# Joining small-matmul bursts in slice 1 of a chunked linear attention with a two-layer MoE: one core of a Trainium2 chip

## The chip, the core and the metric

The kernel runs on one core of one Trainium2 chip. The metric is the device time of one execution in microseconds, the median of several runs. The engines are TensorE (PE for matmuls, PEld for weight loads), VectorE (DVE), ScalarE (ACT), GpSimd (POOL) and SyncE (SP), whose queue issues all DMAs.

## What is computed

Cut to what matters; all data are float32.

```python
# q, k, v: (4, 8, 768, 64), lam: (8,), blocks of 64 positions
for b in range(12):
    intra = (qb @ kb.T * Dmask) @ vb            # Dmask: lam ** (i - j) below the diagonal
    inter = (qb * lam ** (pos + 1)) @ kv_state
    out[b] = intra + inter
    kv_state = lam ** 64 * kv_state + (kb * lam ** (63 - pos)).T @ vb
x = out, as (3072, 512)
g = relu(x @ w_in) ** 2                          # w_in: (512, 2048)
y = g @ w_out                                    # w_out: (2048, 512)
```

## The kernel before

**Chunks and slices.** The 3072 tokens are 24 chunks t of 128 (two blocks of one batch entry for all 8 heads, 6 chunks to a batch entry). Four chunks make a slice m of 512 tokens. For a slice the MoE runs over 16 pieces f of the hidden width: `hidden` multiplies, `positive` and `square` (ScalarE) take relu and square, `rest` (VectorE) gets the square's lower half, and `project` adds the piece into four accumulators. To keep the accuracy each operand is split into an upper half that fp32r holds and a lower half, and three products are added: 12 matmuls of 128x128 by 128x512 for `hidden`, 12 for `project`. A stretch of the loop is named here by the chunks whose attention it does: slice 1 is the loop at m = 0, in which the MoE of the first four chunks runs beside the attention of chunks 4 to 7; slice 2 is the loop at m = 1, with the attention of chunks 8 to 16 beside it. The last slices use fewer products and their own loop.

**Attention of a chunk** is made of small matmuls of 64x64: `scores` (32), `news` (32, what the chunk adds to the state, 16 for the last chunk of a batch entry) and `result` (64, of the masked scores with v and of q with the state). Beside them: `prep_k` and `prep_q` (GpSimd, L492 and L487) scale k and q, `masked` (VectorE, L498 whole or L505 in halves) multiplies the scores by the mask, `fade` (ScalarE, L539) and `advance` (VectorE, L329) or `state` (L521) carry the state on in a ring of three slots, `copy_qx` and `copy_vx` (ScalarE) move rows across, and `attend` with `split` (L593 and L594) puts a result into upper and lower halves for the next slice.

**The step of slice 1.** Each chunk has four steps f, step = f % 4. In step 0 `look` issues scores and news of chunk t = 4 + f // 4 behind the projection, in step 1 they are masked and the state is advanced, in step 2 `result` is issued between the hidden product and the projection, and `attend` follows. Both use a pool of two PSUM banks (`ps_a`). In slice 2 `burst` does scores of t, result of t - 1 and news of t in one run of small matmuls, with two banks of its own (`ps_b`) and a third from the pool of the hidden products (`ps_h`, 2 banks); `keep` takes the result out in two pieces.

**The weights** are rounded on the fly in slice 1, a unit u = f + 2 (two blocks of 128x512) in a step: `first` (ScalarE, L234 and L239), `clamp` (L247), `shift` (L251), `sign` (L258), `rounded` (L264) on VectorE, then in the next step `upper` (ScalarE, L273) and `lower` (L278). Unit f + 1 must be there for the hidden product f + 1. In steps 1 and 2 VectorE does half of `lower` and GpSimd the other (L281), behind a tiny copy `turn` (L285) that waits for VectorE's half. `wload` (L220) issues a unit's loads three units ahead; a unit's raw space is free after its rounding.

**Order.** Nothing reorders: each engine, and SyncE's queue of DMAs, works in the order in which the body issues. One step of slice 1 issues on VectorE: masking and the first state block (step 1), clamp, shift, sign, lower, the second state block (step 1), rounded, rest, and the attention's lower half (step 2).

Of the kernel before, what the change touches and what calls it, by code (L numbers as in the profile page):

```python
# [7 lines left out]
F32 = mybir.dt.float32  # L8
# [35 lines left out]
def body(ctx: ExitStack, tc: tile.TileContext, qT, kT, kvq, lam, w, out):  # L44
# [52 lines left out]
    chunk = {}  # L97

    def place(t):
        if t in (2, 3):  # L100
            x = wk.tile([P, KT * C, 4], F32, name=f"lent{t}", tag=("xh", "xl")[t - 2])
            x = x.rearrange("p a b -> p (a b)")
        else:
            x = sets[t % 2 if t == 1 or 2 * G < t < SOLO else 0].bitcast(F32)
        c = chunk[t] = {}
        for i, n in enumerate(("k", "v", "q", "kf") if t < 2 * G else ("k", "q", "kf", "v")):
            c[n] = x[:, i * DM : (i + 1) * DM]
        c["all"] = x[:, 0 : 3 * DM]
        if t >= 2 * G:
            c["kq"] = x[:, 0 : 2 * DM].rearrange("p (a b) -> p a b", a=2)  # L110
        if t > SOLO and t % 2:
            c["v"] = v_other
# [363 lines left out]
        return o  # L476

    def keep(t, o):
        x = by_pair(held[t // G % 2], t)
        for y in range(2):  # L480
            nc.scalar.copy(x[:, y], o[y].rearrange("p (a i) -> p a i", a=2))

    def prep_q(t):
        n = slice(0 if t % NCB else 1, 2)
# [7 lines left out]
        nc.gpsimd.tensor_tensor(out=x, in0=x, in1=y.broadcast_to([P, NPR, 2, D]), op=ALU.mult)  # L492

    def masked(t):
        a = a_of[t] = a_last[0] if t > (PLAIN + 2) * G else wk.tile([P, 2, 2, 2, L], F32, name="a", tag="a")
        x, w_ = sc_of.pop(t), mask.rearrange("p j a i -> p j (a i)")
        if t < 2 * G:
            V.tensor_tensor(  # L498
                out=a.rearrange("p j b a i -> p j b (a i)"),
                in0=x.rearrange("p j (b n) -> p j b n", b=2),  # L500
                in1=w_.unsqueeze(2).broadcast_to([P, 2, 2, 2 * L]), op=ALU.mult,
            )
            return
        for j in range(2):
            V.tensor_tensor(  # L505
                out=a[:, j].rearrange("p b a i -> p b (a i)"),
                in0=x[j].rearrange("p (b n) -> p b n", b=2),
                in1=w_[:, j].unsqueeze(1).broadcast_to([P, 2, 2 * L]), op=ALU.mult,
            )
# [17 lines left out]
            else:  # L527
                nc.scalar.copy(new, u)

    faded = {}  # L530

    def fade(t, b):
        n = 2 * t + b
        if b == 0:
            faded[t] = wk.tile([P, 2, 4, D], F32, name="faded", tag="a")
        if n % (2 * NCB) and b < len(u_of[t]):
            old = before_block(n).rearrange("p a j d -> p (a j) d")
            for g in range(4):
                nc.scalar.activation(faded[t][:, b, g], old[:, g], AF.Identity, scale=fd[:, g : g + 1])  # L539

    def advance(t, b):
        if b < len(u_of[t]):
            n = 2 * t + b
            new = before_block(n + 1).rearrange("p a j d -> p (a j d)")
            if n % (2 * NCB):
                add(new, u_of[t][b], faded[t][:, b].rearrange("p g d -> p (g d)"))
            else:
                V.tensor_copy(new, u_of[t][b])
        if b:
            del u_of[t], faded[t]  # L550

    def result(t, banks, begun=(), keys=range(2)):
        g = Group(banks, begun, keys)
# [368 lines left out]
    ps_acc = ctx.enter_context(tc.tile_pool(name="ps_acc", bufs=G, space=PSUM))  # L922

    prev = None
    for m in range(PLAIN):
        if m == 0:
            new_x(1)
        else:
            middle.close()
            ps_b = ctx.enter_context(tc.tile_pool(name="ps_b", bufs=1, side="right", space=PSUM))  # L930
            held += [
                wk.tile([P, KT, N], F32, name=f"held{k}", tag=n) for k, n in enumerate(("xh", "xl"))
            ]
        for f in range(NF):
            h = hidden(m, f, *xs_of[m])
            if m == 0:
# [1 line left out]
                step = f % 4  # L938
                u_ = f + 2
                if step == 2:  # L940
                    o = two_banks(ps_a, "att")
                    result(t, of(o))
                    if t + 1 < 2 * G:
                        load(t + 1)
                        load_vx(t + 1)
                    else:
                        for n in (t + 1, t + 2):
                            load_kq(n)
                            load_v(n)
# [46 lines left out]
            else:  # L996
                t = 2 * G + f
                if f == 0:
                    prep_k(t)
                if f <= 2 * G:  # L1000
                    x = burst(t, f > 0, True, lambda: positive(h))
                    rest(m, f, h, square(h))
                else:
                    squared(m, f, h)
                if 1 <= f <= 2 * G:
                    keep(t - 1, x)
                if f <= 2 * G:
                    masked(t)
                    state(t)
                    if f:  # L1010
# [4 lines left out]
                    prep_k(t + 1)  # L1015
                    copy_vx(t)
                if f - 1 in SUMS:
# [3 lines left out]
                if f <= 2 * G:  # L1021
                    copy_qx(t)
                if f == 2 * G + 1:
                    fetch(0)
# [5 lines left out]
            prev = (m, f)  # L1030

    temp = wk.tile([P, 4, DM], F32, name="temp", tag="xl")
    v_other = wk.tile([P, DM], F32, name="v", tag="a")
    a_last = [wk.tile([P, 2, 2, 2, L], F32, name="a", tag="a")]
    for n in range(2, RING):
        fetch(n)
    for d in range((NM - PLAIN) // 2):
# [97 lines left out]
```

## Time and profile before

| | us |
|---|---|
| median of 3 runs | 585.13 (584.63 to 586.6) |
| profiled execution | 585.56 |
| its span, first to last instruction | 583.8 |
| TensorE busy | 574.4 |
| VectorE busy | 318.9 |
| ScalarE busy | 315.6 |
| GpSimd busy | 81.2 |

Busy time is a sum over the span; a stage in which one engine is full can hide in it. In the order of time a line gives the start, the time from the first start to the last end, engine, line, operation, tiles, shape and count; consecutive records of an engine overlap a little, so that what one costs its engine is read from its start to the next one's. Idle time of an engine before an instruction, with what ended it, stands in brackets; an instruction that was issued and could not yet begin is shown as longer, not as idle time before it. The mean granted TensorE clock is 0.991.

### The profile page before, as it was taken

What the parts mean: (1) busy time and instruction counts of PE and PEld (TensorE: products, weight loads), DVE (VectorE), ACT (ScalarE), POOL (GpSimd) and SP (SyncE); (2) the same over time, 40 slices, a digit from 0 to 9 for tenths busy, and PEclk for the clock granted to TensorE, in tenths of its full rate; (3) what the DMA queues carried; (4) which work ended last, traced back from release to release, by engine and by line L of the source; (5) the groups of instructions that cost most, each with busy time, mean ns of one, the idle gap of its engine ahead of it and who ended that gap; (6) DMA issues with size and microseconds to landing.
All of it is one profiled execution on the core that took longest, in us unless ns stands there. A gap on an engine that the chain in (4) does not pass through costs nothing.

```text
span 583.8 us, 12761 instructions
## 1 busy us (share of the span) xinstructions
PE 574.4 (98%) x5240; PEld 471.4 (81%) x5240; DVE 318.9 (55%) x586; ACT 315.6 (54%) x578; POOL 81.2 (14%) x94
## 2 busy tenths in 40 slices
PE   8899999999999999999999999999999999999997
PEld 5787888888888888888888888888888888888885
DVE  6889999936868676533444333446433333334222
ACT  4589988845656555545655444634344444444221
POOL 7302332331323100011111101000000000000000
PEclk9799999999999999999999999999999999999999
DMA  8667667145998943856555563300354444411001
GB/s 333 224 213 248 227 215 253 61 146 200 300 369 258 349 151 107 274 164 181 183 165 154 151 184 94 122 1 0 118 152 127 126 126 125 120 46 73 1 0 72
DMA packets 51273, 93.62 MB, mean 160 GB/s; under 512 B 4624, under 2 KB 19472, under 8 KB 51216
## 3 DMA queue, kind: packets, MB, share of 16 engines
q1 hardware_dynamic: 51216, 92.82, 49.0%
q8 instruction: 41, 0.67, 0.4%
q14 instruction: 16, 0.13, 0.1%
HBM read 71.83 MB, written 20.97 MB: 159 GB/s over the span
## 4 chain that ended last, share of the span: by engine, by line
PE 98%; DVE 0%; issue 0%; ACT 0%; POOL 0%; DVEq 0%; POOLq 0%
PE h L754 26%; PE acc L648 16%; PE h L612 15%; PE acc L649 15%; PE acc L653 15%; PE h L415 4%; PE b L415 2%; PE att L415 2%; PE att L81 1%; PE open L415 1%; PE h L608 1%; DVE st L521 0%; PE h L366 0%; PE h L378 0%; DVE r L657 0%
## 5 line engine op out<-in xcount | busy, mean ns | idle before, releaser
L648 PE MATMUL acc<-wh,gh 128*128 128x512 f32 x336 | 132.9, 395 | 0.0
L653 PE MATMUL acc<-wh,gl 128*128 128x512 f32 x336 | 131.0, 390 | 0.0
L649 PE MATMUL acc<-wl,gh 128*128 128x512 f32 x336 | 130.9, 390 | 0.0
L648 PEld LDWEIGHTS acc<-wh,gh 128*128 128x128 f32 x336 | 63.0, 188 | 13.8
L653 PEld LDWEIGHTS acc<-wh,gl 128*128 128x128 f32 x336 | 63.1, 188 | 13.3
L649 PEld LDWEIGHTS acc<-wl,gh 128*128 128x128 f32 x336 | 63.1, 188 | 12.6
L633 DVE TENSOR_TENSOR gl<-h,gh 128x512 fp32r<-128x512 f32 x48 | 33.1, 689 | 71.7 <-ACT h L628 71.7
L619 ACT ACTIVATE h<-h 128x512 f32<-128x512 f32 x48 | 28.0, 584 | 77.8 <-PE h L612 44.0
L329 DVE TENSOR_TENSOR temp<-h,temp 128x512 f32<-128x512 f32 x48 | 33.0, 688 | 56.9 <-PE h L754 46.9
L754 PE MATMUL h<-wh,ring 128*128 128x512 f32 x224 | 60.0, 390 | 0.0
L619 ACT ACTIVATE temp<-temp 128x512 f32<-128x512 f32 x16 | 10.1, 632 | 88.6 <-DVE temp L329 88.6
L487 POOL TENSOR_TENSOR qs<-set,qpow 128x512 f32<-128x512 f32 (+1 forms) x21 | 26.5, 1263 | 169.1 <-PE b L415 157.6
L754 PEld LDWEIGHTS h<-wh,ring 128*128 128x128 f32 x224 | 42.0, 188 | 9.0 <-DVE r L329 0.4
L329 DVE TENSOR_TENSOR r<-h,temp 128x512 f32<-128x512 f32 x24 | 16.6, 692 | 34.3 <-PE h L754 33.1
L633 DVE TENSOR_TENSOR gl<-r,gh 128x512 fp32r<-128x512 f32 x24 | 16.6, 691 | 32.9 <-ACT gh L786 32.9
L754 PE MATMUL h<-wl,ring 128*128 128x512 f32 x112 | 34.5, 389 | 0.0
L612 PE MATMUL h<-xh,wh 128*128 128x512 f32 x120 | 33.4, 401 | 0.7 <-ACT xh L593 0.7
L612 PE MATMUL h<-xh,wl 128*128 128x512 f32 x120 | 33.1, 398 | 0.0
L612 PE MATMUL h<-xl,wh 128*128 128x512 f32 x120 | 32.2, 390 | 0.0
L786 ACT CAST gh<-r 128x512 fp32r<-128x512 f32 x24 | 14.9, 621 | 30.0 <-PE acc L649 30.0
L623 ACT ACTIVATE gh<-h 128x512 fp32r<-128x512 f32 x48 | 28.8, 600 | 1.4
L628 ACT ACTIVATE h<-h 128x512 f32<-128x512 f32 x48 | 28.5, 594 | 0.0
(209 smaller groups left out, 1120.9 us busy)
## 6 DMA issues: line engine op xcount, KB each, us to landing
ring<-wd SPq DMA_DIRECT2D x56, 256.0 KB, 2.8
raw<-in_w SPq DMA_DIRECT2D x22, 512.0 KB, 4.7
set<-in_kvq SPq DMA_DIRECT2D x16, 512.0 KB, 3.9
wd<-hl SPq DMA_DIRECT2D x16, 512.0 KB, 5.3
set<-in_kT SPq DMA_DIRECT2D x22, 256.0 KB, 5.0
set<-in_w SPq DMA_DIRECT2D x10, 512.0 KB, 5.1
set<-in_kvq SPq DMA_DIRECT2D x6, 768.0 KB, 6.5
wh<-wd SPq DMA_DIRECT2D x14, 256.0 KB, 2.8
```

What stands on the lines that cost most here:

```text
L329: lambda o, x, y, op=op: V.tensor_tensor(out=o, in0=x, in1=y, op=op)
L415: nc.tensor.matmul(self.banks[row][rows[col], at : at + D], lhsT, rhs, start=key not in self.begun, stop=stop, skip_group_check=True,)
L487: nc.gpsimd.tensor_tensor(out=z, in0=x, in1=w_, op=ALU.mult)
L612: nc.tensor.matmul(h, wt[:, w_in(f), kt * P : (kt + 1) * P], x[:, kt], start=k == 0, stop=k == 11)
L619: nc.scalar.activation(h, h, AF.Relu)
L623: nc.scalar.activation(gh, h, AF.Square)
L628: nc.scalar.activation(h, h, AF.Square)
L633: V.tensor_tensor(out=gl, in0=r, in1=gh.bitcast(F32), op=ALU.subtract)
L648: nc.tensor.matmul(accs[m][i], gh[:, cs], wh[:, j], start=f == 0, stop=False)
L649: nc.tensor.matmul(accs[m][i], gh[:, cs], wl[:, j], start=False, stop=False)
L653: nc.tensor.matmul(accs[m][i], gl[:, cs], wh[:, j], start=False, stop=end)
L754: nc.tensor.matmul(bank, w[:, kw * HALF + kt * P : kw * HALF + (kt + 1) * P], x_slot(2 * c + kt, kx), start=first and q == 0, stop=q == 5, ...
```

## The change

Slice 1 gets `burst` from chunk 5 on: in step 2 of chunk t one burst holds scores of t + 1, result of t and news of t + 1, and the last one takes chunk 8 out of slice 2, which then begins with chunk 9. `look` remains for chunk 4. The pool `ps_b` is opened at f = 2. Masking of t + 1 moves into step 2 and is done in halves; the mask's tile `a` becomes a single one from chunk 4 on. The state is faded straight into its new slot (steps 3 and 0) and added there. `prep_q` of t + 1 moves to step 2, `prep_k` to step 1; chunk 5 is loaded in step f = 1, later chunks in step 2 of the chunk two before, and v of the odd chunks has a tile of its own. `rest` stands ahead of `rounded` in steps 1 and 2. `upper` goes ahead of the burst's ScalarE instructions in step 2.

```diff
+        if t > G and t % 2 and (t < 2 * G or t > SOLO):
+            c["v"] = v_other[0]
...
     def keep(t, o):
+        o = [x.rearrange("p (a i) -> p a i", a=2) for x in o]
+        if t < 2 * G:
+            xh, xl = (by_pair(x, t) for x in xs_of[1])
+            for y in range(2):
+                nc.scalar.copy(xh[:, y], o[y])
+            for y in range(2):
+                sub(xl[:, y], o[y], xh[:, y].bitcast(F32))
+            return
...
     def masked(t):
-        a = a_of[t] = a_last[0] if t > (PLAIN + 2) * G else wk.tile([P, 2, 2, 2, L], F32, name="a", tag="a")
+        a = a_of[t] = a_last[0] if t >= G else wk.tile([P, 2, 2, 2, L], F32, name="a", tag="a")
...
-        if t < 2 * G:
+        if t <= G:
...
     def fade(t, b):
...
-                nc.scalar.activation(faded[t][:, b, g], old[:, g], AF.Identity, scale=fd[:, g : g + 1])
+                nc.scalar.activation(new[:, g], old[:, g], AF.Identity, scale=fd[:, g : g + 1])
...
-                add(new, u_of[t][b], faded[t][:, b].rearrange("p g d -> p (g d)"))
+                add(new, u_of[t][b], new)
...
                 if step == 2:
-                    o = two_banks(ps_a, "att")
-                    result(t, of(o))
-                    if t + 1 < 2 * G:
-                        load(t + 1)
-                        load_vx(t + 1)
-                    else:
-                        for n in (t + 1, t + 2):
-                            load_kq(n)
-                            load_v(n)
-                if step == 1:
+                    if f == 2:
+                        middle.close()
+                        ps_b = ctx.enter_context(
+                            tc.tile_pool(name="ps_b", bufs=1, side="right", space=PSUM)
+                        )
+                    upper(u_ - 1)
+                    x = burst(t + 1, True, True, lambda: positive(h))
+                if f == 1:
+                    load_kq(t + 1)
+                    load_v(t + 1)
+                    wload(u_ + 2)
                     masked(t)
                     advance(t, 0)
...
                 if f > 1:
-                    upper(u_ - 1)
+                    if step != 2:
+                        upper(u_ - 1)
                     lower(u_ - 1, step in (1, 2))
                 if f == 1 or f and step in (0, 3):
                     turn(u_ - 1)
-                if step == 1:
+                if step == 2:
+                    prep_q(t + 1)
+                    if t + 1 < 2 * G:
+                        load_vx(t + 1)
+                    load_kq(t + 2)
+                    load_v(t + 2)
+                    if t + 1 == 2 * G:
+                        load_kq(t + 3)
+                if f == 1:
                     fade(t, 1)
                     advance(t, 1)
-                if f == 0:
+                if step == 3:
+                    fade(t + 1, 0)
+                    advance(t + 1, 0)
+                if step == 0 and f:
+                    fade(t, 1)
+                    advance(t, 1)
+                if f == 0 or step == 1:
                     positive(h)
-                    gh = square(h)
-                    rest(m, f, h, gh)
+                if f == 0 or step in (1, 2):
+                    rest(m, f, h, square(h))
                 if u_ < NLOT:
                     rounded(u_)
-                    wload(u_ + 3)
-                if step == 0 and f:
-                    prep_q(t)
-                if step == 3 and t + 1 < 2 * G:
-                    prep_k(t + 1)
-                if f:
+                    if f:
+                        wload(u_ + 3)
+                if step == 1 or f == NF - 1:
+                    prep_k(t + 1 if step == 1 else t + 2)
+                if f and step not in (1, 2):
                     positive(h)
-                    gh = square(h)
-                    rest(m, f, h, gh)
-                if step == 1:
+                    rest(m, f, h, square(h))
+                if f == 1:
                     copy_qx(t)
                 if step == 2:
-                    attend(t, o)
+                    keep(t, x)
+                    masked(t + 1)
+                if step == 3:
+                    copy_qx(t + 1)
...
-                if step == 0:
+                if f == 0:
                     look(t)
                     fade(t, 0)
             else:
-                t = 2 * G + f
+                t = 2 * G + 1 + f
...
-                if f <= 2 * G:
-                    x = burst(t, f > 0, True, lambda: positive(h))
+                if f < 2 * G:
+                    x = burst(t, True, True, lambda: positive(h))
```

## Rows read from the trace of the kernel before

**Rows 1.** The page: TensorE's busy time (us, share of the span, instructions), and VectorE's busy tenths in 40 equal slices of the span.

```profile
PE 574.4 (98%) x5240; PEld 471.4 (81%) x5240; DVE 318.9 (55%) x586; ACT 315.6 (54%) x578; POOL 81.2 (14%) x94
...
DVE  6889999936868676533444333446433333334222
```

**Rows 2.** The busy time of each engine from 26.50 to 195.14 us, slices 1 and 2 of the loop: the sum over the stretches, and the mean of the 15 stretches.

```profile
sum 168.64, PE 168.61 PEld 137.93 DVE 140.18 ACT 126.47 POOL 48.42; mean PE 11.24 PEld 9.20 DVE 9.35 ACT 8.43 POOL 3.23
```

**Rows 3.** TensorE's order of time: the first four matmuls of hidden products, f = 6 to 10 of slice 1 and f = 3 and 4 of slice 2. A step lasts from one such row to the next.

```profile
66.18 1.07 PE L612 MATMUL h<-xh,wh 128*128 128x512 f32 x4
...
72.94 1.07 PE L612 MATMUL h<-xh,wh 128*128 128x512 f32 x4
...
78.38 1.07 PE L612 MATMUL h<-xh,wh 128*128 128x512 f32 x4
...
85.01 1.19 PE L612 MATMUL h<-xh,wh 128*128 128x512 f32 x4
...
90.58 1.07 PE L612 MATMUL h<-xh,wh 128*128 128x512 f32 x4
...
149.10 1.07 PE L612 MATMUL h<-xh,wh 128*128 128x512 f32 x4
...
156.79 1.07 PE L612 MATMUL h<-xh,wh 128*128 128x512 f32 x4
```

**Rows 4.** VectorE's order of time, f = 10 (a step that shares lower) and the full lower of f = 11 with the rounding behind it; last, ScalarE's second square of f = 10.

```profile
92.98 0.68 DVE L247 TENSOR_SCALAR A<-A 128x1024 f32<-128x1024 f32 x1
93.69 0.69 DVE L251 TENSOR_SCALAR A<-A 128x1024 uint32<-128x1024 uint32 x1
94.42 1.22 DVE L258 SCALAR_TENSOR_TENSOR A<-set,A 128x1024 uint32<-128x1024 uint32 x1
95.56 0.68 DVE L278 TENSOR_TENSOR wl<-third,wh 128x512 fp32r<-128x512 f32 x1
96.16 1.22 DVE L264 CUSTOM_DVE_ANT_0 A<-set,A 128x2048 uint16<-128x2048 uint16 x1
97.30 0.68 DVE L633 TENSOR_TENSOR gl<-h,gh 128x512 fp32r<-128x512 f32 x1
97.89 0.68 DVE L594 TENSOR_TENSOR xl<-att,xh 128x512 fp32r<-128x512 f32 x1
...
101.12 1.22 DVE L278 TENSOR_TENSOR wl<-A,wh 128x1024 fp32r<-128x1024 f32 x1
102.26 1.22 DVE L264 CUSTOM_DVE_ANT_0 A<-raw,A 128x2048 uint16<-128x2048 uint16 x1
...
94.61 0.59 ACT L628 ACTIVATE h<-h 128x512 f32<-128x512 f32 x1
```

**Rows 5.** The order of time at the start of slice 1: VectorE's lower half of unit 4 and TensorE's fourth hidden product, upper and lower weights; the squares' lower half of f = 1, and the first matmuls of the result of chunk 4.

```profile
53.46 1.22 DVE L278 TENSOR_TENSOR wl<-A,wh 128x1024 fp32r<-128x1024 f32 x1
...
53.78 1.07 PE L612 MATMUL h<-xh,wh 128*128 128x512 f32 x4
54.73 1.21 PE L612 MATMUL h<-xh,wl 128*128 128x512 f32 x4
...
44.69 0.68 DVE L633 TENSOR_TENSOR gl<-h,gh 128x512 fp32r<-128x512 f32 x1
...
44.36 0.27 PE L415 MATMUL att<-a,set 64*64 64x64 f32 x2
```

**Rows 6.** The order of time in slice 2: masking in halves (VectorE) and the scaling of q (GpSimd).

```profile
132.21 0.41 DVE L505 TENSOR_TENSOR a<-h,mask 128x256 f32<-128x256 f32 x1
132.54 0.41 DVE L505 TENSOR_TENSOR a<-b,mask 128x256 f32<-128x256 f32 x1
...
138.38 1.29 POOL L487 TENSOR_TENSOR qs<-set,qpow 128x512 f32<-128x512 f32 x1 [9.65 <-PE b L415]
```

**Rows 7.** VectorE and GpSimd in order of time: f = 9, where a state addition stands between lower and rounding, and f = 8, where GpSimd's scaling of q falls beside the squares' lower half.

```profile
89.72 0.42 DVE L329 TENSOR_TENSOR st<-att,faded 128x256 f32<-128x256 f32 x1
90.06 2.39 DVE L264 CUSTOM_DVE_ANT_0 third<-raw,third 128x2048 uint16<-128x2048 uint16 x1
...
89.94 0.17 POOL L285 COPY mark<-wl 1x1 f32<-1x1 f32 x1 [4.12 <-DVE wl L278]
90.08 1.29 POOL L281 TENSOR_TENSOR wl<-A,wh 128x512 fp32r<-128x512 f32 x1
...
85.00 0.68 DVE L633 TENSOR_TENSOR gl<-h,gh 128x512 fp32r<-128x512 f32 x1
...
85.09 0.73 POOL L487 TENSOR_TENSOR qs<-set,qpow 128x256 f32<-128x256 f32 x1
```

**Rows 8.** The same view: the scaling of k and the clamp behind it at f = 11, and the mark of f = 1 with the sign behind it.

```profile
103.48 1.05 POOL L492 TENSOR_TENSOR set<-set,near 128x512 f32<-128x512 f32 x1
...
103.99 1.09 DVE L247 TENSOR_SCALAR third<-third 128x1024 f32<-128x1024 f32 x1
...
41.45 0.58 POOL L285 COPY mark<-wl 1x1 f32<-1x1 f32 x1 [18.34 <-DVE wl L278]
...
42.09 1.23 DVE L258 SCALAR_TENSOR_TENSOR A<-set,A 128x1024 uint32<-128x1024 uint32 x1
```

**Rows 9.** SyncE's queue in order of time, the weight loads from 30.45 us, and a line of the page's DMA issues (KB each, median us from issue to landing).

```profile
30.45 8.39 SPq L220 DMA_DIRECT2D raw<-in_w  x4
...
set<-in_kvq SPq DMA_DIRECT2D x16, 512.0 KB, 3.9
```

More of the change, by code (lines that the diff above doesn't have):

```diff
@@ L96, in body @@
     qpow = const.tile([P, NPR, L], F32, name="qpow")
-    chunk = {}
+    chunk, v_other = {}, [None]
     def place(t):
@@ L110, in place @@
             c["kq"] = x[:, 0 : 2 * DM].rearrange("p (a b) -> p a b", a=2)
-        if t > SOLO and t % 2:
-            c["v"] = v_other
+        else:
+            c["kq"] = x[:, 0 : 3 * DM].rearrange("p (a b) -> p a b", a=3)[:, 0:3:2]
+        if t > G and t % 2 and (t < 2 * G or t > SOLO):
+            c["v"] = v_other[0]
         c["v_flat"] = c["v"]
@@ L478, in keep @@
     def keep(t, o):
+        o = [x.rearrange("p (a i) -> p a i", a=2) for x in o]
[6 more added lines that the diff above has]
+            return
         x = by_pair(held[t // G % 2], t)
         for y in range(2):
-            nc.scalar.copy(x[:, y], o[y].rearrange("p (a i) -> p a i", a=2))
+            nc.scalar.copy(x[:, y], o[y])
     def prep_q(t):
@@ L528, in state @@
                 nc.scalar.copy(new, u)
-    faded = {}
     def fade(t, b):
         n = 2 * t + b
-        if b == 0:
-            faded[t] = wk.tile([P, 2, 4, D], F32, name="faded", tag="a")
         if n % (2 * NCB) and b < len(u_of[t]):
-            old = before_block(n).rearrange("p a j d -> p (a j) d")
+            old, new = (before_block(k).rearrange("p a j d -> p (a j) d") for k in (n, n + 1))
             for g in range(4):
-                nc.scalar.activation(faded[t][:, b, g], old[:, g], AF.Identity, scale=fd[:, g : g + 1])
+                nc.scalar.activation(new[:, g], old[:, g], AF.Identity, scale=fd[:, g : g + 1])
     def advance(t, b):
@@ L549, in advance @@
         if b:
-            del u_of[t], faded[t]
+            del u_of[t]
     def result(t, banks, begun=(), keys=range(2)):
@@ L924, in body @@
     prev = None
+    v_other[0] = wk.tile([P, DM], F32, name="v", tag="a")
+    a_last = [wk.tile([P, 2, 2, 2, L], F32, name="a", tag="a")]
     for m in range(PLAIN):
@@ L928, in body @@
         else:
-            middle.close()
-            ps_b = ctx.enter_context(tc.tile_pool(name="ps_b", bufs=1, side="right", space=PSUM))
             held += [
@@ L966, in body @@
                     turn(u_ - 1)
[L967 removed]
+                if step == 2:
[7 more added lines that the diff above has]
+                if f == 1:
                     fade(t, 1)
                     advance(t, 1)
[L970 removed]
+                if step == 3:
[5 more added lines that the diff above has]
+                if f == 0 or step == 1:
                     positive(h)
[L972 to L973 removed]
+                if f == 0 or step in (1, 2):
+                    rest(m, f, h, square(h))
                 if u_ < NLOT:
                     rounded(u_)
[L976 to L981 removed]
+                    if f:
[3 more added lines that the diff above has]
+                if f and step not in (1, 2):
                     positive(h)
[L983 to L985 removed]
+                    rest(m, f, h, square(h))
+                if f == 1:
                     copy_qx(t)
                 if step == 2:
[L988 removed]
+                    keep(t, x)
+                    masked(t + 1)
+                if step == 3:
+                    copy_qx(t + 1)
+                if f == NF - 1:
+                    copy_vx(t + 1)
+                    fade(t + 1, 1)
+                    advance(t + 1, 1)
                 if u_ + 1 < NLOT:
@@ L1014, in body @@
                         load_kq(t + 2)
-                    prep_k(t + 1)
+                    if t + 1 < SOLO:
+                        prep_k(t + 1)
                     copy_vx(t)
+                else:
+                    squared(m, f, h)
                 if f - 1 in SUMS:
@@ L1020, in body @@
                     S = w_sums(SUMS.index(f))
-                if f <= 2 * G:
+                if f < 2 * G:
                     copy_qx(t)
@@ L1032, in body @@
     temp = wk.tile([P, 4, DM], F32, name="temp", tag="xl")
-    v_other = wk.tile([P, DM], F32, name="v", tag="a")
-    a_last = [wk.tile([P, 2, 2, 2, L], F32, name="a", tag="a")]
     for n in range(2, RING):
```

8 lines of the change are left out of this document (1 added, 7 removed).

## The prediction

> **What bounds the kernel now.** I read the page's shares first [rows 1]: TensorE is busy 98% of the span, and in slices 4 to 8 of the 40, which are 44 to 117 us, VectorE shows a 9 throughout. Then the stretches from 26.5 us on [rows 2]: of 168.64 us TensorE is busy for 168.61, so behind the opening it waits for nothing that a record shows, and every microsecond of its instruction stream is a microsecond of the span. What it spends on a step is read from the starts of the hidden product's first matmuls [rows 3]. A plain step takes 78.38 - 72.94 = 5.44 us, a step with a chunk's result 72.94 - 66.18 = 6.76, that is 1.32 more. A step with scores and news takes 85.01 - 78.38 = 6.63, and its tail slows the next step to 90.58 - 85.01 = 5.57, together 1.32 more as well. A joint burst of slice 2 takes 156.79 - 149.10 = 7.69, that is 2.25 more. So two separate groups cost 2.64 us where one burst costs 2.25.
>
> The third view is VectorE's order of time in slice 1, and it is the one that decides. Its 9s stand for instructions back to back; in its steps [rows 4] clamp takes 0.71 us (start to next start), shift 0.73, sign 1.14, a half lower 0.60, a full lower 1.14, rounding 1.14, the squares' lower half 0.59: a plain step is 5.45 us of VectorE against 5.44 of TensorE. It has nothing to give. The tightest place is the fourth hidden product [rows 5]: the weights' lower half for it is written from 53.46 to 54.68, and its matmuls that read it begin at 54.73, where four matmuls at the plain pace (5.44 / 24 = 0.227 us each) after 53.78 would have put them at 54.69. Slack there is nil.
>
> **The change, part by part.**
>
> *Merging on TensorE.* Four pairs are joined (results of chunks 4 to 7 with scores and news of 5 to 8), chunk 8's being taken from slice 2: 4 x (2.64 - 2.25) = 4 x 0.39 = 1.56 us less. As TensorE is the whole chain this comes off the end, if VectorE keeps up.
>
> *VectorE's own work.* Masking in two halves is 2 x 0.33 = 0.66 for 0.60, the attention's lower half in two pieces the same by the nearest row [rows 6]: 0.12 more for a chunk. The state's in-place addition costs what it did (0.34, [rows 7]). A cycle of four steps is then 4 x 4.31 (clamp, shift, sign, rounding, squares) + 2 x 1.14 + 2 x 0.60 (lower) + 0.66 + 0.66 + 2 x 0.34 = 22.72 us. TensorE's cycle becomes 4 x 5.44 + 2.25 = 24.01. That leaves 1.29 us for everything in which VectorE waits.
>
> *The squares' lower half ahead of rounding.* This is where I expect the loss. In the steps that share lower with GpSimd, GpSimd does a mark copy and then its half of 1.29 us, both behind VectorE's half. Where rounding follows at once, that mark is held until rounding is over. Where an instruction that reads PSUM lay between, GpSimd got in: mark 89.94, half 90.08 to 91.37, and the rounding issued at 90.06 took 2.39 instead of 1.22 us [rows 7]. An instruction like the squares' half leaves GpSimd free: its product at 85.09 ran beside the one at 85.00, and neither was slowed [rows 7]. The change puts just such an instruction, 0.59 long, between lower and rounding in two steps of four. Rounding would be issued at 89.72 + 0.59 = 90.31 of that stretch and still end at 92.45, so it takes 2.14, which is 0.92 too long. Twice a cycle: 1.84. The wait on ScalarE that the move adds is nothing: the squares there end at 95.20, a microsecond before VectorE comes to them at 96.24 [rows 4].
>
> *GpSimd's scaling of k* moves from the step after the burst to the step before it, behind the shared half in GpSimd's queue. Before, it ran beside the squares and held up the clamp issued at 103.99, which took 1.09 us for 0.68 [rows 8], 0.41 more. Now rounding, clamp, shift, sign and lower follow it without a PSUM instruction between. It costs nothing if it finds a gap, at most its own length, 1.05. That a waiting GpSimd instruction gets in between two such VectorE instructions is shown by the mark at 41.45, which ended at 42.03, between shift and sign [rows 8]. So I take 1.02. The scaling of q, 1.29 us long [rows 6], queues behind the shared half in the burst's step; if rounding gets in first it lies beside masking and the lower halves (1.32 us, PSUM), and costs 0; if not, 1.25. I take 0, since rounding has been waiting when the half ends.
>
> Sum of a cycle: 22.72 + 1.84 + 1.02 = 25.58 against 24.01, so TensorE waits 1.57 us in a whole cycle, and 1.57 - 0.34 = 1.23 in the one of chunk 5, which has a single state addition.
>
> *The start of the slice, chunk 5 sooner.* In step 1 GpSimd now scales chunk 5's k right behind the mark that ends at 42.03; sign was to start at 42.09. If the product goes first, sign waits 1.0; if sign goes first, it runs beside the two PSUM instructions that follow, and costs rounding 0.2. I take 0.6. Then in step 2 rounding loses 0.92, masking has moved ahead of the fourth lower half (0.66), the pieces add 0.10: 2.28 us later than 54.68. TensorE comes 2.25 - 1.32 = 0.93 later by itself, so it waits 1.35. From the fourth lower half to the fifth VectorE needs 5.45 + 0.34 = 5.79 against 5.44: 0.35 more. The burst needs a third bank of the hidden pool, and so the squares' half of step 1 (45.37 before, [rows 5], 1.13 sooner by the move and 0.6 later by the collision, 44.84) before it starts at 44.36: 0.5 us, part of the same 1.35.
>
> By the Trainium skill, SBUF — State Buffer, section "SBUF: two separate sides", VectorE and GpSimd arbitrate for one pair of ports, an instruction holds it to its end, and VectorE instructions with two SBUF inputs contend as well. The blocked rounding of [rows 7] agrees; no row shows sign blocked. By the page sign would wait the whole 1.0, and the sum below would be 0.4 higher.
>
> *Queues.* On SyncE chunk 5's three loads now stand ahead of a weight load that waited until 38 us anyway (four loads held from 30.45 for 8.39 us, [rows 9]), so they start near 32.5 and land, at some 4 us each [rows 9], before 40. Later loads of k and q wait for the scaling of q in the burst's step and hold the next weight piece back by a microsecond or two; that piece is read two steps later: 0, and a microsecond if the cover is gone. On ScalarE the mark copy that waits for the scores, with the squares queued behind it, and the copies in two pieces fit: ScalarE is busy for 126 of 169 us [rows 2]. The single mask tile makes masking wait for the result, which ends ahead of the squares: 0. Fading straight into the state writes a slot whose last reader is the burst just done: 0.
>
> **Sum.** Gain 1.56; waits 1.35 + 0.35 + 1.23 + 1.57 = 4.50. Net 2.94 us slower. Behind chunk 8 the weights' pieces run out and nothing is given back in slice 2. The profiled execution took 585.56 us (span 583.8), 0.43 above the median of 585.13; the sum goes on the median: 588.1. With 0 to 1.0 on the first sign instead of 0.6, and 0.3 either way for what I rounded, the likeliest case lies between 587.2 and 588.8.
>
> **The rivals.** What a measurement of this kernel can tell from no change is about 0.3%, 1.76 us.
> 1. *The gap stays shut.* If GpSimd's mark does not get in during the squares' half (it reads one operand from SBUF), rounding is not blocked. Place: between lower and rounding, steps 1 and 2. Then a cycle is 22.72 + 1.02 = 23.74, below 24.01, and TensorE waits only at the start, 0 to 1.0. It decides as soon as a cycle's waits on GpSimd stay under 1.29. Result: -1.56 to -0.5, 583.6 to 584.6. Against it: the product at 85.09; for it: marks held to the end of rounding wherever that followed at once. 0.25, mostly within 0.3%.
> 2. *Only the shared half blocks.* The scaling of k finds its gap: a cycle is 24.56, waits are 0.2 to 0.55 a cycle beside 1.7 at the start: some 2.5 in all, net +0.9, 586.0. 0.16.
> 3. *The scaling of q goes ahead of rounding too*, as the half followed the mark at 90.08 while rounding was about to be issued: 1.25 more in three steps, net +6.7, 591.8. 0.14.
>
> **How the numbers follow.** The forecast has 0.45, rivals 0.25, 0.16 and 0.14. Slower by over 0.3%: all of rival 3, nearly all of the forecast's case, little of rival 2: 0.56. Faster by over 0.3% needs more than the whole gain of 1.56: 0.08, out of rival 1. Within: 0.36. The range, 583.5 to 591.0, holds rival 1's full gain and the forecast, and leaves out rival 3's end.
>
> **What would show it.** Steps of 7.69 in slice 1 at the bursts and one group of small matmuls less in slice 2 show the gain. Roundings near 2.1 us in steps 1 and 2 behind the squares' half show the block; a k scaling amid VectorE's clamp or rounding the second. Then TensorE's hidden products should pause ahead of their second group of four, by 0.3 to 0.8 us, at products 4, 5, 8, 9, 12, 13, and at the burst of step 2. Roundings of 1.22 throughout, or no pause on TensorE with long ones, would make it wrong.

## The result, and the profile after

589.83 us, median of five runs (589.05 to 590.4), against 585.29 for five of the kernel before: the ratio is 1.0071, 95% interval 1.0055 to 1.0087. The profiled execution took 589.96 us with a span of 588.1, where the profile before had 583.8, so its span is 4.3 us longer.

The page's shares come first: TensorE's busy time and VectorE's tenths.

```profile
PE 575.4 (98%) x5240; PEld 471.2 (80%) x5240; DVE 323.8 (55%) x587; ACT 318.4 (54%) x594; POOL 79.6 (14%) x94
...
DVE  6789999974767777534344333447433333334222
```

TensorE is at 98% as in [rows 1], and the page shows nothing lost there. VectorE's work is 4.9 us more (323.8 for 318.9), though the change gave it next to no work: most of it is time in which its instructions were held up, as the rows below show. Over the stretch of [rows 2] (26.50 to 195.00 us) TensorE is now busy for 164.65 us of 168.50, where it was busy for all but 0.03. The next view says where. It is TensorE's order of time: the first matmuls of the hidden products of f = 2 to 8 of slice 1, between them two rows that waited, and last the first product of slice 2.

```profile
40.81 1.07 PE L618 MATMUL h<-xh,wh 128*128 128x512 f32 x4
...
44.68 0.27 PE L417 MATMUL h<-set 64*64 64x64 f32 x1 [0.99 <-DVE gl L639]
...
49.61 1.21 PE L618 MATMUL h<-xh,wh 128*128 128x512 f32 x4
...
55.23 1.07 PE L618 MATMUL h<-xh,wh 128*128 128x512 f32 x4
...
56.70 1.20 PE L618 MATMUL h<-xh,wl 128*128 128x512 f32 x4 [0.41 <-DVE wl L280]
...
61.39 1.07 PE L618 MATMUL h<-xh,wh 128*128 128x512 f32 x4
...
67.20 1.07 PE L618 MATMUL h<-xh,wh 128*128 128x512 f32 x4
...
75.27 1.07 PE L618 MATMUL h<-xh,wh 128*128 128x512 f32 x4
...
80.71 1.07 PE L618 MATMUL h<-xh,wh 128*128 128x512 f32 x4
...
131.57 1.07 PE L618 MATMUL h<-xh,wh 128*128 128x512 f32 x4
```

A burst's step without waits is 7.69 us and a plain one 5.44 [rows 3]. These steps take 8.80, 5.62, 6.16, 5.81, 8.07 and 5.44: 1.11, 0.18, 0.72, 0.37, 0.38 and 0 too long. The later ones go on so (f = 8 to 14: 0.34, 0.37, 0.95, 0, 0.36, 0.32, 0.73; the burst of f = 10 is smaller, as chunk 6 begins a batch entry, and takes 7.46 without waits, as the like burst of slice 2 did before, from 164.48 to 171.94). Together TensorE loses 5.83 us in slice 1, by the starts of its products; only a part of it stands as idle time in the view, the rest in rows that are shown as longer or in small gaps. I measure the whole as one **stretch**, from the product of f = 2 in slice 1 to the first of slice 2: 131.57 - 40.81 = 90.76 us. Before it took 126.95 - 41.55 = 85.40 (the kernel before, TensorE's order of time):

```profile
41.55 1.07 PE L612 MATMUL h<-xh,wh 128*128 128x512 f32 x4
...
126.95 1.07 PE L612 MATMUL h<-xh,wh 128*128 128x512 f32 x4
```

With chunk 8's scores and news in it (1.32) and four pairs joined (1.56 less) it would be 85.2.

The rows that the waits lead to are in VectorE's order of time, here at f = 1, in step 2 of chunk 4 (f = 2) and in step 1 of chunk 5 (f = 5):

```profile
41.65 2.04 DVE L260 SCALAR_TENSOR_TENSOR A<-set,A 128x1024 uint32<-128x1024 uint32 x1
...
48.27 0.69 DVE L280 TENSOR_TENSOR wl<-A,wh 128x512 fp32r<-128x512 f32 x1
48.87 0.69 DVE L639 TENSOR_TENSOR gl<-h,gh 128x512 fp32r<-128x512 f32 x1
49.47 2.13 DVE L266 CUSTOM_DVE_ANT_0 A<-raw,A 128x2048 uint16<-128x2048 uint16 x1
51.52 0.41 DVE L331 TENSOR_TENSOR xl<-h,xh 128x256 fp32r<-128x256 f32 x1
...
67.88 2.11 DVE L266 CUSTOM_DVE_ANT_0 A<-raw,A 128x2048 uint16<-128x2048 uint16 x1
69.92 1.55 DVE L249 TENSOR_SCALAR third<-third 128x1024 f32<-128x1024 f32 x1
```

and in GpSimd's at the same places:

```profile
41.56 1.05 POOL L502 TENSOR_TENSOR set<-set,near 128x512 f32<-128x512 f32 x1
49.09 0.18 POOL L287 COPY mark<-wl 1x1 f32<-1x1 f32 x1 [6.47 <-DVE wl L280]
49.23 1.29 POOL L283 TENSOR_TENSOR wl<-A,wh 128x512 fp32r<-128x512 f32 x1
50.48 2.28 POOL L497 TENSOR_TENSOR qs<-set,qpow 128x512 f32<-128x512 f32 x1
...
68.88 2.04 POOL L502 TENSOR_TENSOR set<-set,near 128x512 f32<-128x512 f32 x1
```

The reader is to see pairs. The sign at 41.65 (2.04 for 1.23) has the scaling of k from 41.56 beside it. While the squares' half runs at 48.87 GpSimd gets its mark in (49.09) and its half of lower (49.23 to 50.52), and the rounding issued at 49.47 takes 2.13. In step 1 of chunk 5 it is the same at 67.88, and there the scaling of k was issued at 68.88 and waited for rounding to end, then got in ahead of the clamp at 69.92, which took 1.55 for 0.68.

### The profile page after: what moved, and what is told of

Same layout as the page of the kernel before. It is cut to its first block, busy times and chain, and to the rows that moved or that the text cites. A ratio compares the mean times of both kernels' runs of the same rounds, so it can differ in the third digit from the quotient of the medians.

```text
span 588.1 us, 12793 instructions
## 1 busy us (share of the span) xinstructions
PE 575.4 (98%) x5240; PEld 471.2 (80%) x5240; DVE 323.8 (55%) x587; ACT 318.4 (54%) x594; POOL 79.6 (14%) x94
## 4 chain that ended last, share of the span: by engine, by line
PE 81%; DVE 10%; issue 5%; DMA 2%; ACT 1%; POOL 1%; SPq 0%; POOLq 0%
PE h L760 26%; PE acc L654 13%; PE acc L659 13%; PE acc L655 13%; PE h L618 8%; PE h L417 4%; DVE A L266 2%; PE b L417 2%; DVE gl L639 1%; PE att L81 1%; DMA set<-in_w 1%; DMA set<-in_kvq 1%; DVE third L266 1%; DVE A L249 1%; DVE A L253 1%
## 5 line engine op out<-in xcount | busy, mean ns | idle before, releaser
L625 ACT ACTIVATE h<-h 128x512 f32<-128x512 f32 x48 | 27.9, 582 | 68.5 <-PE h L618 34.9
L497 POOL TENSOR_TENSOR qs<-set,qpow 128x512 f32<-128x512 f32 (+1 forms) x21 | 29.9, 1426 | 169.5 <-PE b L417 157.8
L502 POOL TENSOR_TENSOR set<-set,near 128x512 f32<-128x512 f32 x22 | 26.6, 1207 | 28.6 <-DMA set<-in_kvq 19.9
```

The costliest lines, as they stand in the source:

```text
L497: nc.gpsimd.tensor_tensor(out=z, in0=x, in1=w_, op=ALU.mult)
L625: nc.scalar.activation(h, h, AF.Relu)
```

## The experiments

Two theories stood. **Theory:** VectorE is full, and what it loses to GpSimd (rounding behind the squares' half, and the scaling of k) becomes TensorE's waits. **Rival:** the merged burst itself is at fault, by its three banks, its relay of marks through ScalarE, or its later result, and the long VectorE rows cost nothing. (The relay: ScalarE's 1x1 copy L472, the mark copy, which the burst's news wait for.) The stretch tells them apart; free of waits it is 84.9 us in the joint kernels (by the control below, 85.15 + 1.32 - 1.56).

**1. Rounding back ahead of the squares in steps 1 and 2.**

```diff
-                if f == 0 or step in (1, 2):
+                if f == 0:
                     rest(m, f, h, square(h))
                 if u_ < NLOT:
                     rounded(u_)
+                if f and step in (1, 2):
+                    rest(m, f, h, square(h))
```

> One part of the change undone: rounding stands ahead of the squares' lower half again in steps 1 and 2; all else as changed. Theory (GpSimd's half holds up rounding because the squares' half lets it in): roundings of 1.22 us in steps 1 and 2 instead of 2.1; GpSimd's half then runs beside the squares, in step 2 at no cost, in step 1 the next clamp waits 0.65 for it and 0.9 for the scaling of k. A cycle of VectorE falls from 25.4 to some 24.3 us against 24.0 of TensorE. Against that the squares end 1.14 later, which the first burst pays in full (its third bank). Sum: 586.5 to 588.0 us. Rival (the burst's third bank is what TensorE waits for, and the squares must be early): later squares cost at every burst, 590.5 us or more.

588.46 us, ratio 1.0044 (1.0028 to 1.006), above the expected 586.5 to 588.0; stretch 88.63, so 2.13 us come back. VectorE's order of time in step 1, then GpSimd's:

```profile
67.50 1.22 DVE L266 CUSTOM_DVE_ANT_0 A<-raw,A 128x2048 uint16<-128x2048 uint16 x1
68.64 0.69 DVE L639 TENSOR_TENSOR gl<-h,gh 128x512 fp32r<-128x512 f32 x1
69.24 2.35 DVE L249 TENSOR_SCALAR third<-third 128x1024 f32<-128x1024 f32 x1
```

```profile
68.72 1.29 POOL L283 TENSOR_TENSOR wl<-A,wh 128x512 fp32r<-128x512 f32 x1
69.98 1.05 POOL L502 TENSOR_TENSOR set<-set,near 128x512 f32<-128x512 f32 x1
```

Rounding is short, and the clamp pays for GpSimd's half and the scaling of k, one behind the other, in its place. The first burst also pays, as its third bank comes free only behind the squares. TensorE's waits of 40 to 140 us for that (us in total, times, longest):

```profile
PE h L417 <- DVE gl L639: 2.2, 1, 2.2
```

The gain is smaller than expected, by these two. So the new order of the squares brings that bank 1.2 us sooner (0.99 for 2.2), at the price of the rounding block.

**2. GpSimd left out.**

```diff
-        if shared:
+        if shared and u == NF - 1:
...
-                    prep_q(t + 1)
...
-                if step == 1 or f == NF - 1:
-                    prep_k(t + 1 if step == 1 else t + 2)
+                if f == NF - 1:
+                    prep_k(t + 2)
```

> Leaves out GpSimd's work beside slice 1: its half of the weights' lower part in six steps, the scaling of k for chunks 5 to 8 and of q for 5 to 8 (those values are not what the reference needs); the order of all other work is that of the changed kernel. Theory: VectorE has 22.7 us of work in a cycle of 24.0, no rounding is over 1.3 us, TensorE waits nowhere in slice 1 and the merge's gain of 1.56 us stands alone: 583.7 us, 583.2 to 584.3. Rival (third bank, or ScalarE's copy ahead of the burst, by themselves): pauses of TensorE at the bursts stay, 586.0 us or more.

Stretch 85.68: 5.1 of the 5.9 us of waits are gone with the burst in place, and the rival can hold for the remaining 0.8 at most. The only wait of TensorE that the view names from 40 to 140 us, a rounding of step 2 behind the squares' half, and a burst's step, f = 6, from its product to the next:

```profile
PE h L417 <- DVE gl L639: 0.2, 1, 0.2
```

```profile
48.75 1.22 DVE L266 CUSTOM_DVE_ANT_0 A<-raw,A 128x2048 uint16<-128x2048 uint16 x1
```

```profile
65.52 1.07 PE L618 MATMUL h<-xh,wh 128*128 128x512 f32 x4
...
73.22 1.07 PE L618 MATMUL h<-xh,wh 128*128 128x512 f32 x4
```

The time missed: 587.01 us, median of twelve (584.39 to 587.66), ratio 1.0015 (1.0001 to 1.0028). The zeros that stand for the left-out halves, which GpSimd writes ahead of the slice, were suspected, and a control put them with the same leave-outs into the kernel before.

**3. The control: the kernel before, GpSimd left out.**

```diff
-        if shared:
+        if shared and u == NF - 1:
...
+    for u in (3, 6, 7, 10, 11, 14):
+        nc.gpsimd.memset(wl[:, 2 * u].bitcast(F32), 0.0)
...
-                if step == 0 and f:
-                    prep_q(t)
-                if step == 3 and t + 1 < 2 * G:
-                    prep_k(t + 1)
```

> Control: the kernel before, leaving out the same work of GpSimd beside slice 1 as the changed kernel without GpSimd's work did (the weights' lower halves, the scalings of k and q for chunks 5 to 7), with the same fills ahead of the slice. TensorE waited for nothing there, so both theories expect the stretch from the second hidden product of slice 1 to the first of slice 2 at 92.0 us, 0.2 less than before. On the whole time: if the fills cost the opening nothing, 585.6 us; if they are what put the changed kernel without GpSimd's work at 587.0 us with a stretch of 92.8, then 587.0 to 588.5 us here too, 1.56 above it less its 0.9 of waits.

588.39 us, ratio 1.0051 (1.0036 to 1.0067), and its stretch 85.15. So the filling costs some 3 us, in the opening. Its trace shows the same block there: the first row is TensorE's wait (total, times, longest), the second is in VectorE's and the third in GpSimd's order of time:

```profile
PE open L415 <- DVE st L521: 2.1, 1, 2.1
```

```profile
23.06 3.71 DVE L247 TENSOR_SCALAR A<-A 128x1024 f32<-128x1024 f32 x1
```

```profile
23.37 2.84 POOL L922 MEMSET wl<- 128x512 f32 x6
```

A clamp of 0.68 us took 3.71: it ended behind GpSimd's scaling of q and all six fills, and the state's update behind it, which TensorE waits for, came late. Not every execution pays this: in the profiled one of experiment 2, which took 584.39 us, the clamp ran ahead of the fills (0.68 at 22.72, fills from 25.50).

Against this control the merge without GpSimd is 0.36% faster (1.0015 / 1.0051), 2.1 us by the ratios, whose intervals are 0.13% and 0.16% to either side; the sum had 1.56. As the fills weigh on both medians by an unknown share of the executions, the two stretches are the better measure: with chunk 8's 1.32 on the control's, 86.47 against 85.68 leaves 0.79 of the 1.56. The rest goes into the waits that remain in experiment 2, nearly all at f = 2, 3 and 5 (0.43, 0.15 and 0.16). The control gives the pair that matters most: GpSimd's work in the stretch cost the kernel before 85.40 - 85.15 = 0.25 us, and the changed one 90.76 - 85.68 = 5.08.

**4. The scaling of k alone left out.**

```diff
-                if step == 1 or f == NF - 1:
-                    prep_k(t + 1 if step == 1 else t + 2)
+                if f == NF - 1:
+                    prep_k(t + 2)
```

> Leaves out the scaling of k for chunks 5 to 8 alone (these k stay unscaled). Theory: sign at the first step takes 1.23 us instead of 2.04 and the clamps behind step 1 take 0.68 instead of 1.55; roundings stay at 2.1. TensorE's waits fall by 0.8 at the start and by 0.8 in each of two or three cycles: 587.0 us, 586.6 to 588.0. Rival (only the shared half matters, a clamp's wait is covered): 589.2 us or more.

587.09 us, as expected, ratio 1.0024 (1.0012 to 1.0036); stretch 88.44, 2.32 us less. The first sign is free (VectorE's order of time):

```profile
40.82 1.23 DVE L260 SCALAR_TENSOR_TENSOR A<-set,A 128x1024 uint32<-128x1024 uint32 x1
```

Roundings stay at 2.04 to 2.14 (one of 1.22, with GpSimd's half falling on the clamp behind it). So leaving out the scaling of k gives back 2.3 of the 5.1 us. Experiment 1 is no clean price of the rounding block beside it: its 2.13 are what is left after the later bank and the longer clamps. That the parts simply add up is not shown.

**5. The kernel before, with only the squares moved ahead of rounding.**

```diff
+                if step in (1, 2):
+                    positive(h)
+                    gh = square(h)
+                    rest(m, f, h, gh)
                 if u_ < NLOT:
                     rounded(u_)
...
-                if f:
+                if f and step not in (1, 2):
                     positive(h)
```

> The kernel before with one part of the change alone: the squares' lower half ahead of rounding in steps 1 and 2, no joint bursts. Theory (the squares' half lets GpSimd in): roundings of 2.1 us in step 2, where they were 1.22, and VectorE's cycle longer by 0.9 - 0.25, so that it overtakes TensorE's 24.2 us; what slack there was (1 to 2 us at the weights' lower half) takes up the first cycles: 585.8 to 587.0 us, and 92.2 to 93.4 us from the second hidden product of slice 1 to the first of slice 2 (92.2 before). Rival (the squares' place costs VectorE nothing): roundings of 1.22 us, 585.3 to 585.8 us.

585.82 us, ratio 1.0019 (1.0009 to 1.0028). The time lies where both ranges meet and decides nothing; the roundings and the stretch do: 87.08, 1.68 more than before. The block comes without any merge (VectorE's order of time, step 2), and reaches TensorE:

```profile
73.17 0.68 DVE L633 TENSOR_TENSOR gl<-h,gh 128x512 fp32r<-128x512 f32 x1
73.78 2.13 DVE L264 CUSTOM_DVE_ANT_0 third<-raw,third 128x2048 uint16<-128x2048 uint16 x1
```

```profile
55.74 1.20 PE L612 MATMUL h<-xh,wl 128*128 128x512 f32 x4 [1.10 <-DVE wl L278]
```

In step 1 rounding took 2.13, 1.80 and 1.80. My figure for the stretch was counted from the product before f = 2 and missed (92.2 to 93.4 expected, 94.80 measured): that step is 7.7 or 6.8 us long, as the opening goes.

**6. relu ahead of upper in step 2**, against the waits on ScalarE's mark copy.

```diff
+                    x = burst(t + 1, True, True, lambda: positive(h))
                     upper(u_ - 1)
-                    x = burst(t + 1, True, True, lambda: positive(h))
```

> The changed kernel with one order turned: in step 2 ScalarE does the burst's relu and its copy behind the scores ahead of the weights' upper half, not behind it. In the changed kernel the upper half waits for the late rounding (1.56 us at 70.03) and TensorE's burst waits for that copy (0.49 us at 97.24, 0.41 at 122.67). Theory (VectorE is the pace, ScalarE only hands its lateness on): the waits at the bursts of f = 10 and 14 go, and the next hidden products wait instead, since VectorE's cycle stays at 25.4 us: 588.8 to 590.0 us, and 97 us from the second hidden product of slice 1 to the first of slice 2 (97.6 in the changed kernel). Rival (ScalarE's order is the cause): 587.8 us or less and under 96 us for that stretch.

589.09 us, as expected, ratio 1.0077 (1.0063 to 1.009); stretch 90.07, 0.7 less than in the changed kernel. TensorE's waits from 40 to 140 us:

```profile
PE h L618 <- DVE wl L280: 1.3, 3, 0.5
PE h L417 <- DVE gl L639: 1.0, 1, 1.0
```

The mark's waits are gone, and hidden products wait for lower weights in their stead. The relay passes VectorE's lateness on and has little of its own: its order gave back 0.7 us.

**7 to 9. Gating GpSimd.** A GpSimd copy that reads a tile of VectorE's holds the scalings back until VectorE instructions run that read PSUM (PSUM instructions from here on); the shared halves return to VectorE, whole. The core of all three:

```diff
+    def gate(x):
+        nc.gpsimd.tensor_copy(mark[:, 3:4], x[0:1, 0:1].bitcast(F32))
...
-                    lower(u_ - 1, step in (1, 2))
+                    lower(u_ - 1)
...
+                if f and step in (0, 2):
+                    gate(cv[u_][2])
+                if step == 2:
+                    prep_q(t + 1)
...
+                if f and step == 0 or f == NF - 1:
+                    prep_k(t + 1 if step == 0 else t + 2)
```

> All of the computation, GpSimd moved out of VectorE's way: VectorE does the whole lower part in steps 1 and 2 (0.54 us more each), and a tiny copy on GpSimd that reads a result of VectorE holds the scaling of k back to the squares of step 0 (for chunk 5: to the stretch behind sign) and the scaling of q to the masking of step 2. Theory: no rounding over 1.3 us; a cycle of VectorE is 22.7 + 1.1 + 0.4 = 24.2 us against 24.0, TensorE waits 0.5 at the first burst, 0.35 behind it and 0.2 to 0.4 in a cycle: 584.6 to 585.6 us. Rival (VectorE's own work is too much whatever GpSimd does): 1.08 us more in a cycle, 590.5 us or more.

588.06 us, ratio 1.0042 (1.003 to 1.0055), a miss; stretch 88.50. Behind the first (1.49 us at 42.79) no rounding is long, but VectorE has now two more halves to do in a cycle (its order of time):

```profile
62.41 1.29 DVE L249 TENSOR_SCALAR A<-A 128x1024 f32<-128x1024 f32 x1
...
65.61 1.22 DVE L280 TENSOR_TENSOR wl<-A,wh 128x1024 fp32r<-128x1024 f32 x1
...
67.34 1.22 DVE L266 CUSTOM_DVE_ANT_0 A<-raw,A 128x2048 uint16<-128x2048 uint16 x1
```

A cycle of TensorE, from the product of f = 6 to that of f = 10, is 24.65 us (65.52 to 90.17) in place of 24.01, with a clamp that still meets the scaling of k (1.29 for 0.68). The next puts step 0's state addition, a PSUM instruction, ahead of that clamp:

```diff
-                    advance(t, 1)
...
+                if f and step == 0:
+                    advance(t, 1)
```

> The gated version with the state addition of step 0 moved behind the squares, so that the scaling of k (1.06 us) falls beside 0.93 us of instructions that read PSUM instead of 0.59; all of the computation is done. Theory: the clamp behind step 0 takes 0.7 to 0.9 us instead of 1.29, VectorE's cycle falls from 24.65 to some 24.1 us against TensorE's 24.0, and of the 0.6 us that TensorE lost in the burst's step of each cycle 0.4 to 0.6 come back: 586.6 to 587.4 us against 588.1, the stretch from the second hidden product of slice 1 to the first of slice 2 at 94.6 to 95.2 us instead of 96.2. Rival (the clamp's wait was covered): no change, 588.0 us and 96 us.

586.94 us, ratio 1.0040 (1.0024 to 1.0055); stretch 88.12. The time is in the expected range, but not the stretch from the second product (95.8 us for 94.6 to 95.2), and the ratio is no better than the 1.0042 of the version before. Clamps were 0.70, 0.95 and 0.96, close to what was expected, but a weight piece came late (ScalarE's order of time, first row, and VectorE's, second fence):

```profile
62.98 1.14 ACT L236 ACTIVATE A<-raw 128x1024 f32<-128x1024 f32 x1 [2.90 <-DMA raw<-in_w]
```

```profile
64.23 0.70 DVE L249 TENSOR_SCALAR A<-A 128x1024 f32<-128x1024 f32 x1 [0.77 <-ACT A L236]
```

Last, the weight loads ahead of the gate, and the squares ahead of sign in step 2, so that the first burst's bank comes free sooner:

```diff
+                    x = burst(t + 1, True, True, lambda: positive(h))
+                    gh = square(h)
                     upper(u_ - 1)
-                    x = burst(t + 1, True, True, lambda: positive(h))
...
+                    if step == 2:
+                        rest(m, f, h, gh)
                     sign(u_)
...
+                if u_ < NLOT and f:
+                    wload(u_ + 3)
+                if f and step in (0, 2):
+                    gate(cv[u_][2])
```

> The gated version with the later state addition, and three orders more: in step 2 ScalarE does relu and squares ahead of the weights' upper half, VectorE the squares' lower half ahead of sign, and SyncE the weight piece ahead of the next chunk's loads (in the version without it ScalarE waited 2.9 us for that piece at f = 5). All of the computation is done. Theory (VectorE's sum, the bank that the squares free, and the one late load are all there is): the bursts' steps take 7.7 to 8.0 us (8.83, 8.62, 7.80 and 7.96 there), TensorE's waits in slice 1 fall from 3.2 to some 1.3 us, the stretch from the third hidden product of slice 1 to the first of slice 2 from 88.1 to 86.0 to 86.6 us, and the time stands 0 to 0.7 us below that of the kernel before: 584.4 to 585.4 us. Rival (something else in the joint bursts of slice 1 costs): 87.5 us or more, 586.5 us or more.

588.81 us, ratio 1.0064 (1.0047 to 1.0081), a miss: stretch 90.54. From 40 to 130 us VectorE and TensorE waited (us in total, times, longest):

```profile
DVE gl L642 <- ACT h L637: 4.5, 4, 1.6
...
PE h L621 <- DVE wl L280: 2.3, 6, 0.6
```

VectorE stood still for ScalarE's squares, 4.5 us in four places, on a cycle with no time to give; no run takes these waits out to test that they are all of it. None of the three beats the kernel before.

**10. The changed kernel once more.**

> The changed kernel once more, on the same chip as the others of this call, for a second trace of it: 589.0 to 590.0 us, 90.3 to 91.2 us from the third hidden product of slice 1 to the first of slice 2 (90.76 in its first trace), roundings of 2.1 us in steps 1 and 2.

589.77 us, ratio 1.0072 (1.0057 to 1.0088); stretch 90.86. The stretch repeats to 0.1 us, while the product of f = 2 starts at 41.83 instead of 40.81: the opening differs by a microsecond between executions, so the stretch, and not the span, is the measure for the reasons here.

## Why the prediction came out as it did

588.1 was predicted, within 587.2 to 588.8 for the likeliest case; 589.8 was measured, inside the range, above that inner one. The mechanism was right: TensorE was late at the products 4, 5, 8, 9, 12 and 13 and at the bursts, as forecast, by 0.32 to 0.72 us at the products, and a cycle of VectorE took 25.44 us (from the rounding at 74.58 to that at 100.02) where the sum had 25.58. But the waits came to 5.83 us instead of 4.50, and slice 2 lost 0.89 that the sum did not have.

- **Merging, 1.56 gained.** A burst's step without waits took 65.52 to 73.22 = 7.70 us in slice 1 too (experiment 2), as the 7.69 of [rows 3]. Right to the step; the waits take more than it gives.
- **Rounding behind the squares, 2.14.** Measured 2.11 to 2.13 in steps 1 and 2 from f = 2 to 13, and 1.21 to 1.22 in steps 3 and 0. Right to 0.03, so rival 1 (the gap stays shut) falls.
- **The scaling of k, 1.02.** Clamps of 1.55 and 1.54 instead of 0.68: 0.87. Rival 2 (it finds a gap) falls.
- **The first sign, 0.6.** 2.04 instead of 1.23: 0.81, inside the 0 to 1.0. By the Trainium skill, SBUF — State Buffer, section "SBUF: two separate sides", an instruction holds the pair of ports that VectorE and GpSimd share to its end. The sign agrees nearly in full: 0.81 of the 0.96 that the scaling at 41.56 still had to run at 41.65.
- **The scaling of q, 0.** It was issued at 50.48, behind the half, was held until rounding ended at 51.60 and ran beside the attention's lower halves and the masking (0.41 each, not slowed). Right; rival 3 falls.
- **The start, 1.35 and 0.35.** Measured 1.11 + 0.18 + 0.72 = 2.01 for f = 2 to 4, and 0.37 for f = 5. Here a term was too small: the first burst's wait for its third bank, 0.5 in the sum, is 0.99. Without the block on the first sign (experiment 4) these three steps wait 0.39 + 0.14 + 0.66 = 1.19, so the sign is worth 0.82 of the 2.01, where 0.6 stood; the other 0.44 is not split further.
- **The cycles of chunks 5 and 6, 1.23 and 1.57.** Measured 1.09 (f = 6 to 9) and 1.63 (f = 10 to 13). Right in size, though some of it is lost at the bursts by the chain below.
- **"Behind chunk 8 the weights' pieces run out and nothing is given back in slice 2."** The sum has nothing for the last burst and nothing for slice 2, and both failed. The last burst's step (f = 14) was 0.73 too long, by a chain that I had priced at nothing (the mark copy and the copies in two pieces "fit: ScalarE is busy for 126 of 169 us"). It is to be seen in the step of f = 10, in ScalarE's order of time and then TensorE's:

```profile
95.48 1.05 ACT L275 CAST wh<-third 128x1024 fp32r<-128x1024 f32 x1 [1.69 <-DVE third L266]
96.43 0.58 ACT L625 ACTIVATE h<-h 128x512 f32<-128x512 f32 x1
97.03 0.15 ACT L472 COPY mark<-b 1x1 f32<-1x1 f32 x1
```

```profile
97.24 0.69 PE L417 MATMUL b<-v,set 64*64 64x64 f32 x30 [0.49 <-ACT mark L472]
```

  A rounding that ends late (95.44) lets upper start late, and relu, the mark copy and the news stand behind it in one row; ScalarE's idle 1.69 shows that its busy share of [rows 2] was no measure of the cover. At f = 14 the same wait is 0.41 of the 0.73. With relu ahead of upper (experiment 6) that step takes 7.69, and TensorE waits elsewhere. The other failure is slice 2, 67.76 us where before less chunk 8 makes 68.19 - 1.32 = 66.87: 0.89 over. Nearly all of it lies in the burst of chunk 15, at f = 6, whose step takes 8.61 us for 7.69 (TensorE's order of time):

```profile
177.58 1.07 PE L618 MATMUL h<-xh,wh 128*128 128x512 f32 x4
...
182.91 0.50 PE L417 MATMUL b<-set 64*64 64x64 f32 x17 [0.66 <-issue]
...
186.19 1.07 PE L618 MATMUL h<-xh,wh 128*128 128x512 f32 x4
```

  "issue" names no releaser. The step of f = 6 takes 7.85 to 8.61 us in the joint kernels profiled, and 7.79 to 8.06 in those with the order of before, where it is the burst of chunk 14 and chunk 15's takes 7.69. By these steps the pause follows the place in the loop rather than the chunk (f = 5 takes up to 8.34 in some joint kernels as well), and the kernel before has a smaller one. No experiment took it up; its cause is open.

The account of the span: -1.56 (merge) + 5.83 (waits) - 0.25 (waits that the stretch before had already, by the control) + 0.89 (slice 2) - 0.74 (a shorter opening, which experiment 10 does not repeat) + 0.11 (behind slice 2) = 4.28, against 4.3.

## What to carry to other kernels

Where an engine has no slack, the order of its instructions matters by what may run on the other engine between them: here a VectorE instruction with one operand in PSUM let a waiting GpSimd instruction in, and the next VectorE instruction on SBUF alone paid for it. Before moving an instruction on a full engine, list what waits on the neighbour at that very place, in both directions; GpSimd's work cost 5.08 us of the stretch here, where it had cost 0.25, and the merge itself was worth 1.56. And a cover is read from the row that feeds the hand-over, not from an engine's busy share.

## What was not expected of the hardware

- A waiting GpSimd instruction got in between two VectorE instructions with no PSUM instruction to open a gap: the scaling of k that waited from 68.88 went ahead of the clamp right behind rounding. But the engines do not simply take turns. That rounding, issued at 67.88, had itself gone ahead of the scaling when GpSimd's half ended, while in experiment 1 the clamp issued at 69.24 was passed by the scaling of k from 69.98, and in experiment 3 one issued at 23.06 by all the fills. What decides the order is not shown.
- Six GpSimd fills ahead of the slice, 2.84 us in all, held one clamp, with the scaling of q ahead of them, for 3 us and moved the opening by about as much (experiment 3), though not in every execution.
- TensorE paused for 0.66 us inside 64x64 matmuls, with no releaser in the trace.
